# Second-layer outer products by Strassen's seven, SiLU kept in float32, and another pace and order in the decode of w_in2

## The chip, the cores and the metric

One core of a Trainium2 chip runs the whole program as one launch. The metric is the device time of one execution in microseconds (us); lower is better. Every execution quoted here is of the full problem.

## What is computed

```
q,k,v: [4, 8, 1152, 64] float32; two weight pairs: w_in [512, 2048], w_out [2048, 512], float64 bits
q_pool = mean of q over pairs of rows                         # 576 query rows per head
x      = softmax(q_pool @ k^T / 8) @ v, heads side by side    # [2304, 512]
h = x @ w_in1;  x = (h * cos(h)) @ w_out1                     # layer 1
h = x @ w_in2;  out = silu(h) @ w_out2                        # layer 2, [2304, 512]
```

All results are float32. The weights arrive as 64-bit floats and are taken apart bit by bit on the chip.

## The kernel before, in words

**Precision.** Every float32 operand of a large product is scaled by a power of two and split into two float16 tiles, high and low. A product then takes three matmuls on TensorE: high by high, high by low, low by high (line 519 on, `g1_unit`).

**Blocks.** The 2304 tokens go through both layers as 9 blocks of 256 tokens. For a block, `g1_unit` makes one of 16 chunks `f` of the hidden layer, 128 x 256, with 12 matmuls of 256 columns; `g1_evac` (line 533) takes two chunks out of PSUM at a time on ScalarE. In layer 1 `g_cos_begin` and `g_cos_end` (lines 544, 556) make h cos h of four chunks with four VectorE instructions, one ScalarE sine and one GpSimd subtraction, and `g2_unit1` (line 578) the outer product. In layer 2 `g_silu` (line 571) splits the SiLU result of four chunks into float16 halves in the tile `gt`, and `g2_unit2` (line 600) does the outer product of chunk `f`: two halves of 128 tokens by three passes, 6 matmuls of 512 columns, 96 for a block. `y_evac2` (line 612) scales the two PSUM banks of 512 columns out and stores them.

**Order of the tail.** While attention's last batch runs, the decode of layer 2's weights begins. `units = layer1()` (line 656) yields once for each chunk of layer 1; for each such unit the tail's loop (line 902 on) takes one step of `wgen2`, the generator that loads, decodes and splits layer 2's weights, until w_in2 is done. Then the loop over the blocks `n` and the chunks `f` of layer 2 begins (some 20 lines from line 935 on): a `g1_unit`, its evacuation, one more step of `wgen2` (now w_out2), a step of the load of the next block, and, 48 chunks behind, one `g2_unit2`. The outer products therefore start with block 3 and the last three blocks of them run alone at the end.

**Weights.** `weight_steps` (line 155) works in pieces of 1024 columns of float64 on each of 128 partitions: 8 pieces of w_in2 and 8 of w_out2. A piece is one DMA, a `decode` (line 191: one ScalarE absolute value, four wide VectorE instructions, at lines 207, 210, 215 and 218) and a `write` (line 232: ScalarE twice, at lines 238 and 239, GpSimd once, at line 240). The piece's scale comes from `scale_steps` (line 79): two tiny VectorE instructions make `mw` (lines 88, 91), one tiny TensorE matmul spreads it over the partitions as `bm` (line 96), and three more VectorE instructions make the scale of it (lines 99, 103, 107).

Instructions of an engine run in the order in which the scheduler, from the program's order and its priorities, has put them into that engine's queue; a waiting instruction holds back all behind it.

## Time and profile before

| | |
|---|---|
| median of 3 runs | 1407.86 us (1405.83 to 1409.97) |
| the profiled execution | 1411.62 us, of which the span is 1409.8 us |
| granted clock, mean | 0.928 |
| TensorE (PE) busy | 1162.9 us, 82% |
| VectorE (DVE) | 996.4 us, 71% |
| ScalarE (ACT) | 767.5 us, 54% |
| GpSimd (POOL) | 567.2 us, 40% |
| tail of layer 1 | about 866 to 1021 us |
| first blocks of layer 2 | about 1021 to 1100 us |
| layer 2, both products | about 1100 to 1340 us |
| outer products alone | about 1340 to 1403 us |

PE busy over the whole span says little: in attention (before about 850 us) several engines share the work, in the tail PE does nearly all of it. The four stretches of the table are read apart. The granted clock is the share of full speed at which TensorE was let run. PEld is TensorE's weight load, which runs beside its matmuls.

### The profile page before, as it was taken

What the parts mean: (1) busy time and instruction counts of PE and PEld (TensorE: products, weight loads), DVE (VectorE), ACT (ScalarE), POOL (GpSimd) and SP (SyncE); (2) the same over time, 40 slices, a digit from 0 to 9 for tenths busy, and PEclk for the clock granted to TensorE, in tenths of its full rate; (3) what the DMA queues carried; (4) which work ended last, traced back from release to release, by engine and by line L of the source; (5) the groups of instructions that cost most, each with busy time, mean ns of one, the idle gap of its engine ahead of it and who ended that gap; (6) DMA issues with size and microseconds to landing.
All of it is one profiled execution on the core that took longest, in us unless ns stands there. A gap on an engine that the chain in (4) does not pass through costs nothing.

```text
span 1409.8 us, 24849 instructions
## 1 busy us (share of the span) xinstructions
PE 1162.9 (82%) x10020; PEld 852.0 (60%) x10020; DVE 996.4 (71%) x1848; ACT 767.5 (54%) x907; POOL 567.2 (40%) x296
## 2 busy tenths in 40 slices
PE   1465356787988778898889889979989999999998
PEld 0243233475676556666667678868878766666643
DVE  7999997778777888977999885997776323223110
ACT  3686487668777678876788775553363111111100
POOL 1577276535755466645666563552321000000000
PEclk9976568699999989998999999999999999999999
DMA  7799789987799999978899964441330000000001
GB/s 232 192 239 209 188 155 204 202 171 135 154 201 174 202 194 211 177 151 181 152 209 184 214 131 91 151 119 46 90 105 32 16 31 30 16 16 16 1 30 30
DMA packets 493074, 186.16 MB, mean 132 GB/s; under 512 B 433056, under 2 KB 467872, under 8 KB 492960
## 3 DMA queue, kind: packets, MB, share of 16 engines
q1 hardware_dynamic: 492960, 184.59, 61.7%
q8 instruction: 78, 1.28, 0.4%
q14 instruction: 36, 0.29, 0.1%
HBM read 66.58 MB, written 9.44 MB: 54 GB/s over the span
## 4 chain that ended last, share of the span: by engine, by line
PE 36%; DVE 25%; ACT 9%; issue 8%; DMA 7%; POOL 2%; SPq 2%; ACTq 0%; DVEq 0%; POOLq 0%
PE h L527 14%; PE o L607 13%; DVE sc L410 5%; PE y L586 5%; DMA hlT<-hl 3%; DVE tt L553 2%; DVE tt L552 2%; POOL hl L429 2%; PE sp L391 2%; ACT hl L424 2%; SPq L431 2%; PE pv L442 2%; DVE gh L567 1%; DVE tt L562 1%; DVE vt L311 1%
## 5 line engine op out<-in xcount | busy, mean ns | idle before, releaser
L429 POOL TENSOR_TENSOR hl<-sc,hl 128x1152 f16<-128x1152 f32 x144 | 367.8, 2563 | 189.9 <-ACT hl L424 110.8
L391 PE MATMUL sp<-kT,qT 128*128 128x512 f16 (+1 forms) x768 | 197.6, 375 | 111.2 <-DVE sc L410 86.5
L527 PEld LDWEIGHTS <-ih 128*128 128x128 f16 x2304 | 225.8, 99 | 64.6 <-issue 12.5
L410 DVE TENSOR_SCALAR_CACHE_REDUCE sc<-sp,psu 128x512 f32<-128x512 f32 (+1 forms) x288 | 229.2, 807 | 40.2 <-PE sp L391 38.8
L540 ACT ACTIVATE hk<-h,ca 128x512 f32<-128x512 f32 x144 | 97.7, 682 | 255.0 <-PE h L527 251.0
L418 ACT ACTIVATE sc<-sc,nb 128x1152 f32<-128x1152 f32 x144 | 180.3, 1252 | 95.2 <-DVE nb L415 80.6
L442 PE MATMUL pv<-vt,hlT 128*128 128x130 f16 (+1 forms) x1440 | 197.2, 239 | 39.6 <-DMA hlT<-hl 33.3
L527 PE MATMUL h<-ys,ih 128*128 128x256 f16 x1152 | 194.8, 273 | 2.9 <-ACT hk L540 2.7
L442 PEld LDWEIGHTS <-hlT 128*128 128x128 f16 (+1 forms) x1440 | 148.6, 111 | 71.0 <-DMA hlT<-hl 45.4
L527 PE MATMUL h<-xT,ih 128*128 128x256 f16 x1024 | 187.1, 276 | 4.7 <-ACT hk L540 3.9
L446 PE MATMUL pv<-vt,hlT 128*128 128x65 f16 (+1 forms) x1440 | 189.5, 209 | 0.0
L607 PE MATMUL o<-oh,gt 128*128 128x512 f16 x576 | 187.9, 379 | 1.0 <-ACT oh L238 0.6
L391 PEld LDWEIGHTS <-qT 128*128 128x128 f16 x768 | 77.9, 110 | 179.2 <-issue 137.1
L424 ACT ACTIVATE hl<-sc 128x1152 f16<-128x1152 f32 x144 | 165.5, 1157 | 18.5 <-DMA xT<-xn 8.9
L586 PE MATMUL y<-gl,oh 128*128 128x256 f16 x576 | 159.4, 277 | 3.7 <-POOL gl L568 3.7
L586 PE MATMUL y<-gh,oh 128*128 128x256 f16 x576 | 159.8, 277 | 2.5 <-ACT y L595 1.7
L586 PE MATMUL y<-gh,ol 128*128 128x256 f16 x576 | 159.7, 277 | 0.0
L527 PE MATMUL h<-ys,il 128*128 128x256 f16 x576 | 157.0, 273 | 0.0
L446 PEld LDWEIGHTS <-hlT 128*128 128x128 f16 (+1 forms) x1440 | 143.7, 108 | 16.2 <-issue 6.7
L527 PE MATMUL h<-xT,il 128*128 128x256 f16 x512 | 141.5, 276 | 0.0
L568 POOL TENSOR_TENSOR gl<-tt,gh 128x1024 f16<-128x1024 f32 x36 | 93.5, 2598 | 110.2 <-DVE gh L567 105.5
L607 PEld LDWEIGHTS <-gt 128*128 128x128 f16 x864 | 84.6, 98 | 81.3 <-issue 2.1
(281 smaller groups left out, 1884.5 us busy)
## 6 DMA issues: line engine op xcount, KB each, us to landing
wst<-in_moe_w_in_dram SPq DMA_DIRECT2D x16, 1024.0 KB, 5.7
wst<-in_moe_w_out_dram SPq DMA_DIRECT2D x16, 1024.0 KB, 6.2
stk<-in_k_dram SPq DMA_DIRECT2D x32, 288.0 KB, 4.0
stv<-in_v_dram SPq DMA_DIRECT2D x32, 288.0 KB, 4.4
stq<-in_q_dram SPq DMA_DIRECT2D x32, 256.0 KB, 3.1
ydr<-y SPq DMA_DIRECT2D x9, 512.0 KB, 3.8
y32b<-ydr SPq DMA_DIRECT2D x9, 512.0 KB, 3.3
out_dram<-osb SPq DMA_DIRECT2D x16, 256.0 KB, 2.1
```

The source lines that it names most:

```text
L391: nc.tensor.matmul(sp[:, o - a:o - a + n], P.qT[e][:, t, :], kT[:, o:o + n], start=(e == 0), stop=(e == 1))
L410: nc.vector.tensor_scalar(out=T.sc[:, a:z], in0=sp, scalar1=T.P.su, scalar2=None, op0=ALU.mult, op1=ALU.min, accum_out=mx[:, x:x + 1],)
L418: nc.scalar.activation(out=T.sc, in_=T.sc, func=AF.Exp, scale=-1.0, bias=nb)
L424: nc.scalar.activation(out=hi, in_=T.sc, func=AF.Copy)
L429: nc.gpsimd.tensor_tensor(out=T.hl[:, 1, :], in0=T.sc, in1=T.hl[:, 0, :], op=ALU.subtract)
L442: nc.tensor.matmul(G.pv[r, T.gi], T.hlT[:, 0, c, r], P.vt[i][:, c], start=(c == 0), stop=(c == KC - 1), skip_group_check=True,)
L446: nc.tensor.matmul(G.pv[r, T.gi, 0], T.hlT[:, 1, c, r], P.vt[i][:, c, 0], start=False, stop=(c == KC - 1), skip_group_check=True,)
L527: nc.tensor.matmul(hp, wt[:, c, f * 128:(f + 1) * 128], xt(c), start=(i == 0), stop=(i == 3 * NC - 1), skip_group_check=True,)
L540: nc.scalar.activation(out=o, in_=blk.hp, func=AF.Copy if first else AF.Silu, scale=blk.c.a[:, g:g + 1])
L568: nc.gpsimd.tensor_tensor(out=G.gl, in0=t, in1=gh, op=ALU.subtract)
L586: nc.tensor.matmul(blk.y[:, oc, :], wt[:, f, oc * 128:(oc + 1) * 128], gt[:, f % 4, :], start=(f == 0 and e == 0 and oc % 2 == 0), stop=(f ...
L607: nc.tensor.matmul(blk.y[i], gt[:, f % 4, i * 128:(i + 1) * 128], wt[:, f, :], start=(f == 0 and e == 0), stop=(f == NF - 1 and e == 2),)
```

## The change

**Outer products.** `g_silu`, `g2_unit2` and `y_evac2` go. The SiLU result now stays in float32, in a tile `gs` where layer 1's weights were (the fourth block's in smaller freed tiles). A block's outer product, 256 tokens by 2048 by 512, is cut in halves on each axis and done with seven products of 128 tokens by 1024 by 256 columns in place of eight: `outer_operand` makes the seven left operands `a11, a12, s2, s1, s3, a22, s4` (sums of quarters of `gs` on VectorE, then a ScalarE copy for the high half and a VectorE instruction for the low half), `outer_steps` does 8 x 3 matmuls of 256 columns for each, 168 for a block, and adds the products up: in PSUM (banks Y, X and W) and with small ScalarE and VectorE instructions into the tile `o`. Five operands are made ahead (`OP_AHEAD`). The first product starts in block 3 at chunk 8 (`G2_AT`), and 14 half products follow for 16 chunks.

**Right operands.** A piece of w_out2 is now a slice of 32 columns from each half of its 512: two DMAs with runs of 256 bytes in place of one with 512. `write_sums` makes seven tiles of sums from it: four GpSimd subtractions of 256 elements, and high and low halves (one ScalarE scaling and four copies, four GpSimd subtractions of 256 or 512 elements) in place of two ScalarE and one GpSimd instruction of 1024 elements.

**Decode.** Of w_in2 one step of `wgen2` is taken for two units of layer 1 in place of one step for one (`W2_EACH`). And `apart` splits `scale_steps`: `mw` is made at once, but the `bm` matmul and what follows come with the next piece.

**Memory.** PSUM's pool `ps_m` has one bank in place of two. The tile of w_out2's last two sums lies where layer 1's `ih1` was.

Order of VectorE in the tail of layer 1, where pieces of w_in2 (`wt`, `wst`, `mw`, `bm`) and groups of layer 1's cosine (`tt`, `hk`, `gh`) alternate. Before:

```order
L99 TENSOR_SCALAR ui2_113<-bm_10688 128x1
L210 TENSOR_SCALAR wt_10724<-wt_10724 128x1024
L88 TENSOR_SCALAR mw_10756<-wm_10723 128x1
L553 SCALAR_TENSOR_TENSOR tt_10981<-tt_10981,hk_10907 128x1024
L103 TENSOR_SCALAR si2_112<-ui2_113 128x1
L215 SCALAR_TENSOR_TENSOR wst_10625<-wst_10625,wt_10724 128x1024
L91 SCALAR_TENSOR_TENSOR mw_10756<-wm_10723,mw_10756 128x1
L567 CAST gh_10826<-tt_10828 128x1024
L107 TENSOR_SCALAR ui2_113<-ui2_113 128x1
L218 SCALAR_TENSOR_TENSOR wst_10625<-wst_10625 128x1024
L562 SCALAR_TENSOR_TENSOR tt_10981<-hk_10907,ck_10333,tt_10981 128x1024
L99 TENSOR_SCALAR ui2_113<-bm_10759 128x1
```

After (line 96 is now 99, 99 is 102, 207 is 230, 210 is 233, 215 is 238, 218 is 241, 552 is 620, 562 is 630, 567 is 635):

```order
L230 TENSOR_SCALAR wt_10957,wm_10956<-wt_10957 128x1024
L635 CAST gh_10768<-tt_10770 128x1024
L233 TENSOR_SCALAR wt_10957<-wt_10957 128x1024
L89 TENSOR_SCALAR mw_11019<-wm_10956 128x1
L630 SCALAR_TENSOR_TENSOR tt_10903<-hk_10839,ck_10328,tt_10903 128x1024
L238 SCALAR_TENSOR_TENSOR wst_10794<-wst_10794,wt_10957 128x1024
L92 SCALAR_TENSOR_TENSOR mw_11019<-wm_10956,mw_11019 128x1
L102 TENSOR_SCALAR ui2_113<-bm_10989 128x1
L620 TENSOR_SCALAR tt_11037<-hk_10973 128x1024
L241 SCALAR_TENSOR_TENSOR wst_10794<-wst_10794 128x1024
L106 TENSOR_SCALAR si2_112<-ui2_113 128x1
```

Before, `bm_10759` is read (last row) five rows behind `mw_10756`, its own piece's. After, the row behind `mw_11019` reads `bm_10989`, which belongs to the piece before.

Order of GpSimd where w_out2's pieces (`wst`) come last. Before, three pieces with layer 1's last groups between them:

```order
L240 TENSOR_TENSOR ol2_10395<-wst_10932,oh2_10394 128x16x64
L240 TENSOR_TENSOR ol2_10395<-wst_11015,oh2_10394 128x16x64
L568 TENSOR_TENSOR gl_11783<-tt_11784,gh_11782 128x1024
L568 TENSOR_TENSOR gl_11896<-tt_11897,gh_11895 128x1024
L240 TENSOR_TENSOR ol2_10395<-wst_12130,oh2_10394 128x16x64
L240 TENSOR_TENSOR ol2_10395<-wst_12211,oh2_10394 128x16x64
```

After, one piece and the start of the next; `ops5` and `ops2` hold the seven sums, and three of the four subtractions of 256 elements stand in one row:

```order
L284 TENSOR_TENSOR wst_12354<-wst_12354 128x256 x3
L275 TENSOR_TENSOR ops5_10389<-wst_12354,ops5_10389 128x16x32
L275 TENSOR_TENSOR ops5_10389<-wst_12354,ops5_10389 128x8x32
L284 TENSOR_TENSOR wst_12354<-wst_12354 128x256
L275 TENSOR_TENSOR ops5_10389<-wst_12354,ops5_10389 128x16x32
L284 TENSOR_TENSOR wst_12457<-wst_12457 128x256 x2
```

One instruction of 1024 elements for a piece has become eight of 256 or 512.

Order of TensorE where the first products come in. Before, chunk 3 of block 3 (`h`) and the first outer products (`o`) alternate:

```order
L527 MATMUL h_12971<-ys_12795,ih2_10392 128x256
L527 LDWEIGHTS il2_10393
L527 MATMUL h_12971<-ys_12795,il2_10393 128x256
L607 LDWEIGHTS gt_12074
L607 MATMUL o_12944<-oh2_10394,gt_12074 128x512
L527 LDWEIGHTS ih2_10392
L527 MATMUL h_12971<-ys_12795,ih2_10392 128x256
```

After, at chunk 8 of block 3, with `op` the left and `ops5` the right operand, and `oy`, `ox` the banks:

```order
L592 MATMUL h_13073<-ys_12853,il2_10388 128x256
L761 LDWEIGHTS op_13131
L761 MATMUL oy_13150<-ops5_10389,op_13131 128x256
L761 LDWEIGHTS op_13131
L761 MATMUL oy_13150<-ops5_10389,op_13131 128x256
L99 MATMUL bm_13923<-ym_13883,mean_72 128x1
L761 LDWEIGHTS op_13134
L761 MATMUL ox_13208<-ops5_10389,op_13134 128x256
```

Two matmuls of 512 columns with one weight load each have become more of 256 columns, each with its own.

The core of the diff:

```diff
-W2_BUFS, W2_PACE, W2_N = 3, 6, 1
+W2_BUFS, W2_PACE, W2_EACH = 3, 6, 2
+G2_AT, OP_AHEAD = 8, 5
...
-    def scale_steps(m, pool, res, top, wide=False):
+    def scale_steps(m, pool, res, top, wide=False, apart=False):
...
             m = w
+            if apart:
+                yield
         bc = pool.tile([128, 2, GW], F32, tag="h", name="bm")[:, 0, 0:4]
         nc.tensor.matmul(bc[:, 0:n], mean, m, start=True, stop=True)
...
+                if w.sums and kind == "o":
+                    n //= 2
+                    st = stage.tile([128, 2, c, n, z], dt, tag="wst", name="wst", bufs=bufs)
+                    for j in range(2):
+                        o = j * (DM // 2) + p * n
+                        eng.dma_start(
+                            out=st[:, j].rearrange("p c f z -> p c (f z)"),
+                            in_=srcs[1][:, o * z:(o + n) * z].rearrange("(c p) f -> p c f", p=128),
+                        )
...
+        def write_sums(p):
+            st = decoded.pop(0)[0]
+            v, f = (st[:, :, :, z] for z in (1, 0))
+            nc.scalar.activation(out=v, in_=v, func=AF.Copy, scale=w.so[:, p:p + 1])
+            b11, b21, b12, b22 = (v[:, i * (NF // 2):(i + 1) * (NF // 2)] for i in range(4))
+            t1, t3, t2, t4 = (f[:, i * (NF // 2):(i + 1) * (NF // 2)] for i in range(4))
+            for o, x, y in ((t1, b12, b11), (t3, b22, b12), (t2, b22, t1), (t4, b21, t2)):
+                nc.gpsimd.tensor_tensor(out=o, in0=x, in1=y, op=ALU.subtract)
+            halves((0, 2), v[:, 0:NF], p)
+            yield
+            halves((2, 1), b22, p)
+            halves((3, 4), f, p)
+            more()
...
-                nc.tensor.matmul(
-                    blk.y[i], gt[:, f % 4, i * 128:(i + 1) * 128], wt[:, f, :],
-                    start=(f == 0 and e == 0), stop=(f == NF - 1 and e == 2),
-                )
...
+        if op == "s2":
+            s1 = mp.p.tile([128, HF, 128], F32, tag="hk", name="s1", bufs=NB_HK)
+            blk.s1 = lambda c, n: s1[:, c:c + n, :]
+            total(blk.s1, a22, a21, ALU.add, g1)
+            total(a21, a11, a21, ALU.subtract, g0)
+            total(a11, blk.s1, a11, ALU.subtract, g0)
+        elif op == "s4":
+            total(a12, a12, a11, ALU.subtract, g1)
...
+            nc.scalar.activation(out=h, in_=x(c, g), func=AF.Copy, scale=blk.c.k)
+            nc.vector.scalar_tensor_tensor(
+                out=l, in0=x(c, g), scalar=blk.c.k, in1=h, op0=ALU.mult, op1=ALU.subtract
+            )
...
+            bank = B.X if op == "a12" else B.W if op in ("s1", "s4") else B.Y
+            start = op in ("a11", "a12", "s1")
...
+            for c in range(HF):
+                for e, wt in ((0, oh), (0, ol), (1, oh)):
+                    nc.tensor.matmul(bank, t[:, e, c, :], wt[:, c, :], start=start, stop=True, skip_group_check=True)
+                    start = False
...
+            if op == "a11":
+                copy(o[:, 0, d0], bank)
+            elif op == "a12":
+                add(o[:, 0, d0], bank)
+            elif op == "s2":
+                copy(o[:, 0, d1], bank)
+            elif op == "s3":
+                copy(o[:, 1, d1], bank)
+                add(o[:, 1, d1], B.W)
+            elif op == "a22":
+                scaled(B, o[:, 1, d0], bank)
+                scaled(B, o[:, 1, d1], o[:, 1, d1])
+            elif op == "s4":
+                add(o[:, 0, d1], bank)
+                for d in (d0, d1):
+                    scaled(B, o[:, 0, d], o[:, 0, d])
...
+            step += 1
+            if step % W2_EACH == 0 and not W2.half:
+                next(wgen2, None)
...
-                if f % 4 == 3:
-                    g_silu(cur, f)
-                pend.append((cur, f, n))
                 next(wgen2, None)
...
-                if len(pend) > (TAIL_G - 1) * NF:
-                    second()
+                if outer is None and n == TAIL_G - 1 and f == G2_AT:
+                    outer = outer_steps(state.mp, opp, W2, blocks, banks, out_dst, OP_AHEAD)
+                if outer is not None:
+                    credit += 14
+                    while credit >= NF:
+                        credit -= NF
+                        next(outer, None)
```

## Rows read from the trace of the kernel before

**Rows 1.** Chain of waits, 850 to 1410 us: start us, us, what

```profile
1076.78 5.24 PE h L527 x48
...
1383.72 20.89 PE o L607 x96
```

**Rows 2.** Busy us (x instructions) by engine and stretch; granted clock; DMA share; GB/s

```profile
866.00:1021.00 155.00, 140.05 (x1239) 122.45 (x1239) 127.53 (x172) 73.77 (x84) 62.57 (x23) 0.97 0.34 97
1021.00:1100.00 79.00, 73.44 (x647) 63.00 (x646) 52.12 (x83) 36.01 (x46) 12.74 (x5) 1.00 0.20 61
1100.00:1340.00 240.00, 240.00 (x1666) 162.57 (x1665) 66.88 (x94) 36.76 (x51) 0.00 (x0) 1.00 0.05 18
...
890.00:942.00 52.00, 42.35 (x366) 36.10 (x364) 52.00 (x74) 27.99 (x31) 22.41 (x8) 0.93 0.32 94
```

**Rows 3.** What PE waited for, 866 to 1021 us: total us, times, longest

```profile
PE bm L96 <- DVE mw L91: 7.9, 3, 6.7
PE h L527 <- ACT hk L540: 2.9, 3, 2.4
```

**Rows 4.** What PE waited for, 1021 to 1130 us

```profile
PE h L527 <- ACT hk L540: 2.7, 3, 1.3
PE bm L96 <- DVE mw L91: 2.0, 1, 2.0
```

**Rows 5.** Timeline of PE: start us, us, work [idle before, releaser]

```profile
927.61 0.58 PE L96 MATMUL bm<-mw,mean 128*128 128x1 f32 x2 [6.71 <-DVE mw L91]
```

**Rows 6.** Busy time by stretch behind that wait, columns as above

```profile
928.00:930.00 2.00, 2.00 (x11) 1.44 (x12) 2.00 (x5) 0.70 (x1) 0.00 (x0) 0.50 0.00 0
930.00:932.00 2.00, 2.00 (x15) 1.59 (x14) 2.00 (x7) 1.16 (x1) 0.00 (x0) 0.72 0.00 0
```

**Rows 7.** DVE by line, 890 to 942 us: xcount, busy us, mean ns

```profile
L562 DVE SCALAR_TENSOR_TENSOR tt<-hk,ck,tt 128x1024 f32<-128x1024 f32 x5 | 10.1, 2012 | 0.0
L210 DVE TENSOR_SCALAR wt<-wt 128x1024 int32<-128x1024 int32 x6 | 8.7, 1444 | 0.0
```

**Rows 8.** Timeline of DVE, one clean row at 930 us

```profile
929.99 0.69 DVE L210 TENSOR_SCALAR wt<-wt 128x1024 int32<-128x1024 int32 x1
```

**Rows 9.** Timeline of POOL, about 1000 us

```profile
999.45 4.68 POOL L240 TENSOR_TENSOR ol<-wst,oh 128x1024 f16<-128x1024 f32 x2 [5.59 <-ACT wst L239]
```

**Rows 10.** Timeline of DVE beside it, and one like it at 990 us

```profile
990.65 1.22 DVE L553 SCALAR_TENSOR_TENSOR tt<-tt,hk 128x1024 f32<-128x1024 f32 x1
...
1002.17 3.04 DVE L553 SCALAR_TENSOR_TENSOR tt<-tt,hk 128x1024 f32<-128x1024 f32 x1
```

**Rows 11.** POOL by line, 1021 to 1100 us

```profile
L240 POOL TENSOR_TENSOR ol<-wst,oh 128x1024 f16<-128x1024 f32 x5 | 12.7, 2554 | 41.7 <-ACT wst L239 41.7
```

**Rows 12.** Timeline of POOL, an undisturbed row near the start

```profile
5.63 1.40 POOL L316 TENSOR_TENSOR stq<-stq 128x576 f32<-128x576 f32 x1 [4.48 <-DMA stq<-in_q_dram]
```

**Rows 13.** ACT by line and shape, 866 to 1100 us

```profile
L595 ACT ACTIVATE y<-y,cy 128x256 f32<-128x256 f32 x16 | 6.4, 476 | 7.6 <-PE y L586 5.2 <-POOL gl L568 2.4
L890 ACT ACTIVATE ys<-y32b,ys 128x1024 f16<-128x1024 f32 x4 | 4.6, 1148 | 0.0
```

**Rows 14.** DVE by line and shape, 1021 to 1410 us

```profile
L575 DVE SCALAR_TENSOR_TENSOR gt<-hk,ck,gt 128x1024 f16<-128x1024 f32 x36 | 46.2, 1282 | 0.9
...
L617 DVE TENSOR_TENSOR osb<-o,cy 128x512 f32<-128x512 f32 x18 | 12.3, 689 | 106.7 <-PE o L607 106.7
```

**Rows 15.** The page's DMA issues: KB each, median us to landing

```profile
wst<-in_moe_w_in_dram SPq DMA_DIRECT2D x16, 1024.0 KB, 5.7
wst<-in_moe_w_out_dram SPq DMA_DIRECT2D x16, 1024.0 KB, 6.2
```

**Rows 16.** Timeline of DVE at the end

```profile
1403.99 1.34 DVE L617 TENSOR_TENSOR osb<-o,cy 128x512 f32<-128x512 f32 x2 [19.68 <-PE o L607]
```

**Rows 17.** Timeline of SP's DMA queue at the end

```profile
1404.71 2.46 SPq L622 DMA_DIRECT2D out_dram<-osb  x4
```

**Rows 18.** The page's groups: PE weight loads of line 527

```profile
L527 PEld LDWEIGHTS <-ih 128*128 128x128 f16 x2304 | 225.8, 99 | 64.6 <-issue 12.5
```

More of the change, by code (lines that the diff above doesn't have):

```diff
@@ L147, in new_w @@
         w.half = False
+        w.sums = sums
         for nm in ("si", "ui", "so", "uo"):
@@ L220, in decode @@
                 )
-                ts.append(st.bitcast(F32)[:, :, :, 1])
+                ts.append(st.bitcast(F32) if w.sums and kind == "o" else st.bitcast(F32)[:, :, :, 1])
+                for g in rest:
+                    next(g)
                 yield
+            for g in rest:
+                run_all(g)
             m1 = m
@@ L226, in decode, with halves @@
                 nc.vector.tensor_reduce(out=m1, in_=m, axis=AX.X, op=ALU.max)
-            for _ in early(scale_steps(m1, pspool(), (s, u), 14, wide), P_CH):
-                pass
+            g = early(scale_steps(m1, pspool(), (s, u), 13 if w.sums and kind == "o" else 14, wide, apart), P_CH)
+            if apart:
+                next(g)
+                scaling.append(g)
+            else:
+                run_all(g)
             decoded.append(ts)
             yield
+        def halves(ops, t, p):
+            o, n = ops
+            f = t.shape[2]
+            for x0, x1, hi, lo in w.ops:
+                y0, y1 = max(o, x0), min(o + n, x1)
+                if y0 >= y1:
+                    continue
+                h, l = (
+                    x[:, y0 - x0:y1 - x0].rearrange("p o c f -> p (o c) f")[:, :, p * f:(p + 1) * f] for x in (hi, lo)
+                )
+                tt = t[:, (y0 - o) * (NF // 2):(y1 - o) * (NF // 2)]
+                nc.scalar.activation(out=h, in_=tt, func=AF.Copy)
+                nc.gpsimd.tensor_tensor(out=l, in0=tt, in1=h, op=ALU.subtract)
+        def write_sums(p):
[11 more added lines that the diff above has]
+            more()
+            yield
         def write(kind, p):
+            if w.sums and kind == "o":
+                yield from write_sums(p)
+                return
             c, n = shape(kind)
@@ L255, in weight_steps @@
                 yield from decode(*pieces[i + ahead])
+            else:
+                finish_scales()
             yield from write(*x)
-        r = npc // NC
+        r = 0 if w.sums else npc // NC
         for e in range(r):
@@ L536, in g1_evac @@
         g = f * w.npc // NF
-        if f % 4 == 1:
-            blk.hk = mp.p.tile([128, 4, GW], F32, tag="hk", name="hk", bufs=NB_HK)
-        o = blk.hk[:, (f % 4) - 1:(f % 4) + 1, :]
+        if first:
+            if f % 4 == 1:
+                blk.hk = mp.p.tile([128, 4, GW], F32, tag="hk", name="hk", bufs=NB_HK)
+            o = blk.hk[:, (f % 4) - 1:(f % 4) + 1, :]
+        else:
+            o = blk.view(f - 1, 2)
         nc.scalar.activation(
@@ L612, in y_evac2, with __init__, view @@
-    def y_evac2(W2, pool, blk, dsts):
-        cy = y_scale(W2, blk.u, W2.uo, "cy0")
-        for i in range(2):
-            o = pool.tile([128, DM], F32, tag="x32_%d" % i, name="osb")
-            np_ = W2.npc
+    class Slot:
+        def __init__(self, parts):
+            self.parts = parts
+        def view(self, c, n):
+            for c0, n0, t in self.parts:
+                if c0 <= c and c + n <= c0 + n0:
+                    return t[:, c - c0:c - c0 + n, :]
+    HF = NF // 2
+    PRODUCTS = ("a11", "a12", "s2", "s1", "s3", "a22", "s4")
@@ new lines, in outer_steps, with prepare, copy, add @@
+    def outer_steps(mp, opp, w, blocks, banks, dsts, ahead_n):
+        seq = [(0, "a11")]
+        for n in range(len(blocks)):
+            seq += [(n, op) for op in ("a12", "s2", "s1", "s3")]
+            if n + 1 < len(blocks):
+                seq.append((n + 1, "a11"))
+            seq += [(n, "a22"), (n, "s4")]
+        todo = list(seq)
+        ready = []
+        def prepare(k):
+            while todo and len(ready) < k:
+                n, op = todo[0]
+                if blocks[n] is None:
+                    return
+                todo.pop(0)
+                ready.append(outer_operand(mp, opp, blocks[n], op))
+        def copy(o, x):
+            nc.scalar.activation(out=o, in_=x, func=AF.Copy)
+        def add(o, x):
+            nc.vector.tensor_tensor(out=o, in0=o, in1=x, op=ALU.add)
+        def scaled(B, o, x):
+            np_ = w.npc
@@ L925, in attention_moe_moe_kernel, with banks @@
         cur = yb.blk
-        pend = []
-        def second():
-            blk, ff, nn = pend.pop(0)
-            g2_unit2(W2, blk, ff, ps_o)
-            if ff == NF - 1:
-                y_evac2(W2, wpool, blk, out_dst(nn))
-        gen = None
+        blocks = [None] * NB
+        def banks(nm, n):
+            if nm == "Y":
+                t = ps_o.tile([128, DM], F32, tag="o%d" % (n % 2), name="oy")
+            elif nm == "X":
+                t = ps_y.tile([128, NC, GW], F32, tag="y", name="ox").rearrange("p c n -> p (c n)")
+            else:
+                t = ps_m.tile([128, DM], F32, tag="w", name="ow")
+            return t[:, 0:DM // 2]
+        outer = None
+        credit = 0
         for n in range(NB):
@@ L955, in attention_moe_moe_kernel @@
                 cur = nyb.blk
-        while pend:
-            second()
+        run_all(outer)
         ctx.enter_context(moe_stack)
```

119 lines of the change are left out of this document (86 added, 33 removed).

## The prediction

> **What bounds the kernel now.** I read the chain of waits first, then busy time by stretch, then who waited for whom inside the stretches that are not full. The chain from 1100 us on is TensorE (PE) and nothing else: its pieces are runs of layer 2's first product, 48 matmuls of 256 columns in 5.24 us, and of the outer product, 96 matmuls of 512 columns in 20.89 us [rows 1]. That is 109.2 ns and 217.6 ns for one, and the first pair of numbers to keep. By stretch, PE is busy 240.00 of 240 us between 1100 and 1340, so there only PE work counts. Between 866 and 1021 it is busy 140.05 of 155, which leaves 15 us idle, and between 1021 and 1100 it is busy 73.44 of 79, which leaves 5.6 [rows 2]. What PE waited for in the first of these is the little matmul `bm` of a weight piece's scale, 7.9 us in 3 waits, one of 6.7, and a free `hk`, 2.9 us [rows 3]; in the second `hk` again, 2.7 us, and `bm`, 2.0 us [rows 4]. A long wait costs twice: behind the 6.71 us wait [rows 5] the granted clock is 0.50 (1.2 of 2.4 GHz) for two us and 0.72 for two more [rows 6], so 2 x 0.50 + 2 x 0.28 = 1.6 us are lost on top. What PE waits for is VectorE (DVE): it is busy all 52.00 us between 890 and 942 [rows 2], and its instructions are stretched there. A decode instruction of line 210 has a mean of 1444 ns [rows 7] against 0.69 us where nothing disturbs it [rows 8]. While GpSimd (POOL) ran two subtractions in 4.68 us [rows 9], DVE's line 553 took 3.04 us instead of 1.22 [rows 10]: the two hold each other up.
>
> **A, the products.** Per block 96 x 217.6 ns = 20.89 us go, and 7 x 8 x 3 = 168 matmuls of 256 columns come. Their nearest row is line 527, of the same shape, types and pattern of one weight load for each matmul: 168 x 109.2 ns = 18.35 us. So a block saves 2.54 us, and nine save **22.9 us**, all of it on the path: the outer products run either where PE is always busy or alone at the end. The weight loads go from one for 512 columns to one for 256; a load takes 99 ns in line 527's groups [rows 18], less than the 109.2 ns of a matmul, and lies beside it there already. Here a rule speaks against the change. The Trainium skill ("TensorE: Matmul & The Clock Gate", section Back-to-back issue gap) gives about 131 ns for a matmul of 512 columns in a stream with a weight load each, and 81 ns for one of 128. By that, as an estimate between its two figures, 256 columns take some 98 ns, and 1512 x 98 ns less 864 x 131 ns makes the products 35 us slower instead. The rows do not agree with it, 217.6 and 109.2 ns, and the measurement decides.
>
> New operands need other engines. A block takes 7 low halves on DVE like line 575's 1282 ns, 4 sums of 1024 elements like the 1.22 us row, and 7 small output instructions of 256 elements at a bit over half of line 617's 689 ns [rows 10, 14], taken as 0.42: 9.0 + 4.9 + 2.9 = 16.8 us, for 18.35 us of PE work. ScalarE (ACT) takes 7 copies like line 890's 1148 ns and 3 of 256 columns like line 595's 476 [rows 13]: 9.5 us. Both fit, DVE not by much. In the stretch to 1340 half of the PE time is the first product's, so there the fit is easy; DVE has 66.88 of 240 us busy now [rows 2]. I cost this work at nothing. Its cover is five operands made ahead; without it every product would show an operand's ACT and DVE time.
>
> **B, the decode of w_in2 and the late scale.** In the order of DVE `bm` is now read one piece behind its `mw`, so PE issues that matmul long after its input is there: the 7.9 us of waits should go, and with them the 1.6 us of clock; a good half of `hk`'s 2.9 could, with about as much of the clock, 1.5 us, behind its wait of 2.4. At most 7.9 + 1.6 + 2.4 + 1.5 = 13.4 us. At least nothing: DVE is full in 890 to 942, and a wait that leaves PE's `bm` can come back at `hk` or `gh`. The two orders differ less than the halved rate says, since both have about one piece for each group of cosine; 9 pieces stand beside 9 groups before, beside 10 after. A tenth of the stretch's DVE work of 52 us is 5 to 6 us. I take 6 us for that and 2 for the clock: **8 us**, nearer the middle than either end, because the wait is surely removed and its cause, a full DVE, only eased.
>
> **C, the new right operands and the first products.** Two rows of the stretch 1021 to 1100 show what changes: the `bm` wait of 2.0 us goes [rows 4], but POOL's work for a piece grows. Now it is one subtraction of 2554 ns [rows 11]. A bare subtraction of 576 elements takes 1.40 us [rows 12], so four of 256 take some 0.7 to 0.9 each and four halves of 256 to 512 some 4.4 in all, 7.2 to 8.3 us for a piece. With 5 such pieces left in that stretch POOL's 12.7 us become 36 to 42, of the 41.7 + 12.7 it has there, so it still fits. But POOL holds up DVE longer, and SP's queue now carries 16 DMAs for w_out2 instead of 8. The first product must have the last piece's sums, and its first operand lies where the last sums' staging was: from that piece POOL's 7 to 8 us and then 1.15 + 1.28 us for the operand. It stands at chunk 8 of block 3 in PE's order, 56 x 12 x 109.2 ns = 73.4 us behind the first matmul of layer 2, where the old one stood at chunk 3. No row shows the price. If all fits, the stretch's idle 5.6 us go but for half a microsecond: -5. If POOL is one and a half pieces late, +12. I take **+3**: the pieces come closely packed, as POOL's fill of 36 to 42 of 54 us says, and half a late piece less the gone `bm` wait is about that.
>
> **D, the end.** Behind the last matmul DVE now multiplies twice, 512 elements each, 1.34 us together [rows 16], and the first store goes out after 0.7. With the change an addition and two scalings of 256 elements stand before the first store, three by 0.42 in a row, about 1.3 us; the stores' own 2.46 us [rows 17] stay. I take **+0.7**, between 0 and +1.2.
>
> **The sum.** -22.9 - 8 + 3 + 0.7 = -27.2. The profiled execution took 1411.6 us, so 1384.4; it lies 3.8 above the median of the runs, 1407.9, to which I refer the forecast: **1381 us**, or 1380.7 before rounding. The ends of the parts give 22.9 + 13.4 + 5 = 41.3 less, 1367, and 22.9 - 12 - 1.2 = 9.7 less, 1398.
>
> **Rivals.**
> *Better than forecast.* The whole 13.4 us of B go, and C brings 4: -22.9 - 13.4 - 4 + 0.7 = -39.6, **1368 us**. For it speaks that the `bm` wait is more than half of the idle time; against it that DVE has no slack there.
> *DVE stays the bound.* The waits only change their name, B is 0, and POOL's sums are late, C is +6: -16.2, **1392 us**. The full 52 us and the stretched instructions speak for it.
> *Short runs.* The rows have w_in2's pieces landing after 5.7 us and w_out2's, with runs of 512 bytes, after 6.2 [rows 15]; runs of 256 bytes have no row. If a piece takes twice 6.2 us, the eight pieces fall behind by up to 50 us, of which the 41.7 us that POOL sits idle there take most: about +8, **1389 us**. The Trainium skill ("DMA: Bandwidth & Descriptors", section Specifications) asks for 512 bytes and more for full rate; no run here shows a shorter run's rate. Against it: two of the three staged pieces are loaded ahead.
> *A wait at every change of product, slower than before.* There are 63 products, and each needs an operand from ACT and DVE and a bank that ACT or DVE has copied out (Y again for `s2`, `s3` and `a22`, W for `s4`, and now one bank in `ps_m`). It decides from 27.2 / 63 = 0.43 us for each. The nearest waits of PE for ACT are 2.7 us in 3 [rows 4], 0.9 each; then 63 x 0.9 = 57 us come on top: **1437 us**. Against it: a product runs 2.62 us, the copy of a bank takes half of one, and Y only gets more added to it.
> *The matmuls are dearer than line 527's.* At 864 x 217.6 / 1512 = 124.3 ns each nothing is left of A and the sum is -4.3, **1404 us**. Only a weight load longer than 109 ns would do it, against 99 in the row.
>
> **How the numbers follow.** I give the forecast 0.59, better 0.08, DVE as bound 0.17, short runs 0.10, a wait at every product 0.04, dearer matmuls 0.02. A measurement here tells from no change what is over 0.3%, 4.2 us, so "faster" ends at 1403.6. The first four cases are faster, though the last two of them together, or with a late start, would reach 1400, so I leave some of them to "same": faster 0.91, same 0.04, slower 0.05. The range takes in the forecast, DVE as bound, short runs and the edge of the better case: 1367 to 1397. It leaves out the two slower rivals and the worst end of C.
>
> **What would show it.** Right: 1512 matmuls of 256 columns at 109 ns in the new products, the last 24 and a half of them (126 half products less the 77 that fit in beside the first product) alone at the end for 64 us without gaps, `bm` waits of under 3 us in all, DVE with some idle time in the tail of layer 1. Wrong: PE idle before the new products that wait for `op` or for a bank, more than 6 us idle where the first of them stands, waits for `hk` and `gh` as long together as `bm`'s were, or w_out2's pieces landing after 9 us or more.

## The result

The changed kernel takes 1397.68 us at the median (1395.49 to 1400.23, 4 runs) against 1407.46 (1405.83 to 1409.97, 4 runs): a ratio of 0.9913 with a 95% interval of [0.9884, 0.9943]. It is faster, by 9.8 us where 27 were forecast, and 0.7 us outside the range of 1367 to 1397. Measured again with more runs it came to 1393.42 us against 1411.69, a ratio of 0.9869 [0.9845, 0.9893], so 18 us; what is known of the difference stands among the experiments. The profiled execution took 1400.23 us, of which the span is 1398.1.

First the same cuts in both traces, at places that mean the same: the end of attention, the last `y` of layer 1, the first outer product, the last first product `h`, the last outer product. Busy time by stretch of the kernel before:

```profile
859.60:1021.20 161.60, 146.65 (x1301) 128.46 (x1300) 133.54 (x191) 75.75 (x88) 64.70 (x24) 0.97 0.33 95
1021.20:1064.30 43.10, 37.54 (x338) 32.77 (x337) 33.65 (x63) 25.16 (x31) 10.62 (x4) 1.00 0.32 96
1064.30:1340.30 276.00, 276.00 (x1973) 192.80 (x1973) 85.15 (x116) 47.61 (x67) 2.12 (x1) 1.00 0.05 18
1340.30:1404.60 64.30, 63.89 (x294) 28.55 (x292) 6.64 (x10) 0.68 (x1) 0.00 (x0) 1.00 0.07 25
```

and of the changed kernel; columns as in [rows 2]:

```profile
865.30:1030.00 164.70, 148.72 (x1308) 130.06 (x1307) 124.27 (x181) 73.97 (x91) 78.01 (x37) 0.97 0.35 87
1030.00:1111.90 81.90, 74.13 (x673) 65.08 (x671) 45.69 (x88) 48.73 (x70) 52.17 (x48) 1.00 0.32 78
1111.90:1327.30 215.40, 215.40 (x1978) 193.07 (x1976) 114.05 (x158) 89.40 (x122) 0.00 (x0) 1.00 0.05 18
1327.30:1393.50 66.20, 65.64 (x600) 58.44 (x598) 42.02 (x67) 26.56 (x42) 0.00 (x0) 1.00 0.08 28
```

Length less PE busy is PE's idle time. Up to the last `y` it was 161.6 - 146.65 = 15.0 us and is 164.7 - 148.72 = 16.0: the stretch that was to give 8 us has become 3.1 us longer, 1.0 of it idle time and 2.1 PE's busy time. Seven more of layer 2's matmuls stand in it, some 0.8 us, and the rest goes with the clock: the mean granted clock is 0.97 in both, but before, 3.3 us of the time at 0.50 (1.2 of 2.4 GHz) lay in PE's idle time, and now PE is busy in all of it. The 2 us that B was to give by the clock did not come. Up to the first product idle time goes from 5.6 to 7.8 us. Then PE is full in both. PE's busy time behind the last `y` falls from 37.54 + 276.00 + 63.89 = 377.4 us to 74.13 + 215.40 + 65.64 = 355.2, by 22.3: that is part A, but for the 0.8 us of those seven matmuls. The end behind the last matmul takes 1398.1 - 1393.5 = 4.6 us in place of 5.2. Together, behind the end of attention: 550.2 us before, 532.8 now, **17.4 less**. But in these two executions attention ended at 859.6 and at 865.3.

What PE waits for up to the last `y`, in the changed kernel:

```profile
PE h L592 <- ACT hk L608: 7.2, 4, 3.6
PE y L647 <- POOL gl L636: 5.2, 3, 3.1
PE bm L99 <- DVE si L106: 1.7, 1, 1.7
PE y L647 <- ACT y L656: 1.0, 1, 1.0
PE bm L99 <- DVE mw L92: 0.8, 1, 0.8
```

Against [rows 3] `bm` fell from 7.9 us to 1.7 + 0.8, as forecast; `hk` rose from 2.9 to 7.2 and `gl` from 2.3 to 5.2. From the last `y` to the first product:

```profile
PE h L592 <- ACT gs L608: 7.2, 8, 1.4
PE bm L99 <- DVE mw L92: 0.6, 1, 0.6
```

The waits of [rows 4] are replaced by eight for `gs`, the evacuation of SiLU.

Where `hk` comes from is read in three timelines about the longest of these waits. PE:

```profile
950.29 0.44 PE L592 MATMUL h<-xT,ih 128*128 128x256 f16 x2 [3.63 <-ACT hk L608]
```

ScalarE, which has to evacuate that `hk`:

```profile
947.46 1.20 ACT L301 ACTIVATE ih<-wst,si 128x1024 f16<-128x1024 f32 x1 [3.81 <-DVE si L106]
948.57 1.10 ACT L229 ACTIVATE wt<-wst 128x1024 f32<-128x1024 f32 x1
949.56 0.68 ACT L608 ACTIVATE hk<-h,ca 128x512 f32<-128x512 f32 x1
```

VectorE:

```profile
946.08 0.15 DVE L102 TENSOR_SCALAR ui<-bm 128x1 f32<-128x1 f32 x1
946.15 1.22 DVE L241 SCALAR_TENSOR_TENSOR wst<-wst 128x1024 int32<-128x1024 int32 x1
947.28 0.15 DVE L106 TENSOR_SCALAR si<-ui 128x1 int32<-128x1 int32 x1
```

The late scale is there: `bm`, of the piece before, is read at 946.08. But the scale `si` is made of it only behind another wide bit instruction, at 947.28; ScalarE's write of that piece (L301) stood waiting for `si` since 943.66; the absolute value of the next decode (L229) follows, then `hk` at 949.56, and PE waits 3.63 us for that. **The wait of PE for a scale has become a wait of ScalarE for the scale made of it, with PE's evacuation queued behind.** The next longest, 2.66 us for `hk` at 936.64, has the same order: ScalarE stood 6.95 us for `si`, while two VectorE instructions ahead of it took 3.08 and 3.15 us in place of 1.2, beside two subtractions on GpSimd. ScalarE's waits for `si` up to the last `y`, before and now:

```profile
ACT ih L238 <- DVE si L103: 7.7, 3, 4.1
...
ACT ih L301 <- DVE si L106: 11.5, 3, 7.0
```

GpSimd's work from the end of attention to the first product, by line and shape:

```profile
L636 POOL TENSOR_TENSOR gl<-tt,gh 128x1024 f16<-128x1024 f32 x13 | 36.3, 2795 | 43.7 <-DVE gh L635 34.5 <-DVE ui L110 7.2 <-DVE mw L89 2.0
L284 POOL TENSOR_TENSOR wst<-wst 128x256 f32<-128x256 f32 x32 | 35.7, 1134 | 32.1 <-ACT wst L280 32.1
L275 POOL TENSOR_TENSOR ops<-wst,ops 128x512 f16<-128x512 f32 x24 | 31.7, 1326 | 3.8 <-ACT ops L274 3.8
...
L275 POOL TENSOR_TENSOR ops<-wst,ops 128x256 f16<-128x256 f32 x8 | 8.3, 1043 | 0.0
```

The eight pieces of w_out2 take 35.7 + 31.7 + 8.3 = 75.7 us, 9.5 each, where its one subtraction took 2.55 before [rows 11]. And ScalarE from the last `y` to the first product:

```profile
ACT ops L274 <- POOL wst L284: 18.0, 9, 3.7
ACT gs L608 <- PE h L592: 6.4, 5, 2.3
```

It waits 18.0 us for GpSimd's subtractions (line 284), at the copy of a high half (line 274), while a `gs` stands behind that copy. One such place, two rows of ScalarE and one of PE:

```profile
1063.43 0.67 ACT L274 ACTIVATE ops<-wst 128x512 f16<-128x512 f32 x1 [3.53 <-POOL wst L284]
1064.00 1.25 ACT L608 ACTIVATE gs<-h,ca 128x512 f32<-128x512 f32 x2
...
1064.72 0.38 PE L592 MATMUL h<-ys,ih 128*128 128x256 f16 x2 [1.38 <-ACT gs L608]
```

### The profile page after: what moved, and what is told of

It is laid out like the page before. It is cut to its first block, busy times and chain, and to the rows that moved or that the text cites. A ratio compares the mean times of both kernels' runs of the same rounds, so it can differ in the third digit from the quotient of the medians.

```text
span 1398.1 us, 26495 instructions
## 1 busy us (share of the span) xinstructions
PE 1145.2 (82%) x10668; PEld 916.7 (66%) x10668; DVE 1065.5 (76%) x1958; ACT 856.6 (61%) x1045; POOL 619.3 (44%) x352
## 4 chain that ended last, share of the span: by engine, by line
PE 31%; DVE 22%; ACT 9%; POOL 9%; issue 8%; DMA 7%; SPq 3%; POOLq 0%; ACTq 0%; DVEq 0%
PE h L592 11%; PE oy L761 7%; DVE sc L475 5%; PE ow L761 3%; PE y L647 3%; DVE tt L621 3%; POOL hl L494 2%; POOL ops L275 2%; DMA hlT<-hl 2%; POOL wst L284 2%; ACT hl L489 2%; PE sp L456 2%; DVE tt L620 2%; PE ox L761 2%; POOL gl L636 2%
## 5 line engine op out<-in xcount | busy, mean ns | idle before, releaser
L592 PE MATMUL h<-xT,ih 128*128 128x256 f16 x1024 | 190.1, 279 | 11.0 <-ACT hk L608 10.4
L761 PEld LDWEIGHTS <-op 128*128 128x128 f16 x1512 | 147.9, 98 | 17.8 <-issue 0.6
L592 PE MATMUL h<-ys,il 128*128 128x256 f16 x576 | 157.0, 273 | 0.0
L647 PEld LDWEIGHTS <-oh 128*128 128x128 f16 x1152 | 113.0, 100 | 20.9 <-issue 4.5
L592 PEld LDWEIGHTS <-il 128*128 128x128 f16 x1152 | 114.0, 99 | 16.7 <-issue 1.5
```

Of the source, the lines that this page charges most:

```text
L592: nc.tensor.matmul(hp, wt[:, c, f * 128:(f + 1) * 128], xt(c), start=(i == 0), stop=(i == 3 * NC - 1), skip_group_check=True,)
L647: nc.tensor.matmul(blk.y[:, oc, :], wt[:, f, oc * 128:(oc + 1) * 128], gt[:, f % 4, :], start=(f == 0 and e == 0 and oc % 2 == 0), stop=(f ...
L761: nc.tensor.matmul(bank, t[:, e, c, :], wt[:, c, :], start=start, stop=True, skip_group_check=True)
```

## The experiments

**Theory Q** is that the gain was given back in queues: GpSimd's sums of w_out2 come ahead of `gl` on GpSimd, and ScalarE's copies, which wait for them, ahead of `hk` and `gs`. **Theory D**, the rival (not part D of the sum): VectorE's load sets the pace of the tail, and a wait taken away only changes its name. All runs at a glance; lengths and idle times from one profile each, cut as above, "behind" from the end of attention to the end of the span, the ratio of the runs against those of the kernel before:

| kernel | attention ends | to last y | PE idle there | PE idle to first product | behind | ratio |
|---|---|---|---|---|---|---|
| before | 859.6 | 161.6 | 15.0 | 5.6 | 550.2 | |
| changed | 865.3 | 164.7 | 16.0 | 7.8 | 532.8 | 0.9913 |
| changed again | 855.7 | 166.4 | 17.7 | 8.3 | 535.1 | 0.9869 |
| e1 decode part alone | 858.9 | 162.4 | 13.8 | 3.0 | 547.4 | 0.9991 |
| e2 pace of before | 861.4 | 164.9 | 16.6 | 7.7 | 533.0 | 0.9875 |
| e3 scale at once | 858.1 | 161.7 | 13.7 | 13.1 | 537.7 | 0.9899 |
| e4 sums on VectorE | 856.1 | 160.7 | 12.4 | 8.9 | 531.7 | 0.9883 |
| e5 no sums | 861.0 | 160.2 | 11.8 | 2.9 | 522.6 | 0.9804 |
| e6 halves later | 856.3 | 163.5 | 15.5 | 8.3 | 533.6 | 0.9890 |
| e7 short decode | 865.6 | 157.0 | 11.6 | 5.0 | 522.0 | 0.9826 |
| e9 scale sooner | 859.7 | 163.3 | 16.2 | 7.8 | 531.5 | 0.9890 |
| e10 e9, highs on VectorE | 858.4 | 164.9 | 19.0 | 7.2 | 535.1 | 0.9890 |
| e11 e9, sums' highs on VectorE | 861.3 | 164.3 | 18.1 | 6.2 | 533.3 | 0.9876 |
| e12 sums on both | 861.5 | 160.8 | 14.0 | 9.6 | 536.0 | 0.9889 |
| e13 short decode, no sums | 861.9 | 154.1 | 9.3 | 1.5 | 514.9 | 0.9779 |
| e14 before, short decode | 861.3 | 158.7 | 12.6 | 2.2 | 542.2 | 0.9942 |

**The changed kernel again.**

> The changed kernel again, unchanged. In seven profiles so far the end of attention lay between 856 and 865 us although its instructions are the same; the changed kernel's own profile had the latest. If that is chance: attention ends at 856 to 861 us, the stretch behind it is again within 1 us of 532.8, and the runs come to 14 to 18 us faster than before. If the change slows attention: it ends at 864 us or later again, 8 to 11 us faster than before.

Attention ended at 855.7 us and the runs came to 18 us less. The same kernel gave 865.3 and 855.7, and over all profiles the end of attention lies between 855.7 and 865.6 us. TensorE's first 5,724 matmuls, most of attention, run in the same order before and after; the last of them starts at 823.3 us in the kernel before, and in the changed one at 828.7 and, this time, at 819.1. So the difference is not the change's; what makes it is not known. Behind attention the two executions are 17.4 and 15.1 us shorter than the kernel before, so the 18 us of this measurement lie nearer to what the change is worth than the 9.8 of the first. Kernels are compared behind attention; there the same kernel gave 532.8 and 535.1, and less than about 3 us tells nothing.

**e1, the decode part alone**, on the kernel before:

```diff
-W2_BUFS, W2_PACE, W2_N = 3, 6, 1
+W2_BUFS, W2_PACE, W2_EACH = 3, 6, 2
...
+            if apart:
+                yield
```

> The kernel before with only the decode part of the change: one step of w_in2's decode for two units of layer 1, and the scale's matmul a piece later; outer products and w_out2 as before. Theory Q (queues: the decode part helps by itself, and what it gains is given back because GpSimd's new sums of w_out2 sit in the queues of GpSimd and ScalarE ahead of layer 1's gl and layer 2's evacuations): PE's idle time between the end of attention and the last y falls from 15 us to 7 to 9, waits for bm under 3 us, the whole 5 to 8 us faster than before. Theory D (VectorE sets the pace of that stretch, the waits only change their names): idle stays at 14 to 17 us, bm's 7.9 us turn up at hk and gl, the whole within 2 us of before.

Behind attention 2.8 us less than before, and a ratio of 0.9991 [0.9975, 1.0008]. PE's waits up to the last `y`:

```profile
PE h L546 <- ACT hk L559: 6.1, 3, 2.7
PE y L605 <- ACT y L614: 5.4, 2, 4.5
PE y L605 <- POOL gl L587: 1.3, 2, 0.9
PE bm L98 <- DVE mw L91: 1.0, 1, 1.0
```

`bm` went from 7.9 us to 1.0; `hk` went from 2.9 to 6.1 and the wait for ScalarE's `y` from 1.0 to 5.4. The longest, 4.5 us for `y`, ends at 954.82. On ScalarE that `y` stands behind a write that waits for `si`:

```profile
952.09 1.23 ACT L255 ACTIVATE ih<-wst,si 128x1024 f16<-128x1024 f32 x1 [2.12 <-DVE si L105]
953.22 1.55 ACT L614 ACTIVATE y<-y,cy 128x256 f32<-128x256 f32 x4
```

That is theory D's picture, in a kernel without w_out2's sums. Part B was small by itself; it wasn't only given back.

**e2 and e3, one part of it undone** in the changed kernel:

```diff
-W2_BUFS, W2_PACE, W2_EACH = 3, 6, 2
+W2_BUFS, W2_PACE, W2_EACH = 3, 6, 1
```

> The changed kernel with one step of w_in2's decode for each unit again. Theory Q: bm's waits stay under 3 us since the scale still comes a piece later; GpSimd's sums of w_out2 come no later, the whole within 3 us of the changed kernel. Theory D: more VectorE work beside each group of cosine: waits for hk and gl together grow from 12.4 us by 3 to 6, the stretch up to the last y as much longer.

```diff
-..., nc.sync, 1, W2_BUFS, 1, 1, True)
+..., nc.sync, 1, W2_BUFS, 1, 1)
```

> The changed kernel with the scale's matmul at once again, the slow pace kept. Theory Q: bm's waits are back at 6 to 9 us in the stretch up to the last y, hk and gl stay at 12, the whole 4 to 7 us slower than the changed kernel. Theory D: bm's waits are back, but hk's and gl's fall by as much; idle time of the stretch 14 to 18 us as in both kernels, the whole within 2 us of the changed kernel.

The pace is worth nothing, 533.0 us: `bm` waits 7.2 us again, `hk` 3.7 in place of 7.2, `gl` 4.6. Both theories missed there, as theory D wanted `hk` and `gl` longer and Q `bm` short. Without the late scale it is 3 to 5 us longer behind attention. Up to the last `y` it is 3 to 5 us shorter; behind it PE waits 6.0 us for one `bm` and 5.3 us for one `ys`, the split of layer 2's input on VectorE, and for `gs` only 1.8. So if the late scale is worth anything in this kernel, it is not where I put it; the runs (0.9899 against 0.9913 and 0.9869) show no difference.

**e4, the sums on VectorE:**

```diff
-                nc.gpsimd.tensor_tensor(out=o, in0=x, in1=y, op=ALU.subtract)
+                nc.vector.tensor_tensor(out=o, in0=x, in1=y, op=ALU.subtract)
```

> The changed kernel with the four subtractions of 256 elements for each piece of w_out2 on VectorE in place of GpSimd. Theory Q: ScalarE's half copies no longer wait 18 us for these subtractions, PE's waits for gs fall from 7.2 us to under 3, those for gl from 5.2 to about 3: 5 to 8 us faster than the changed kernel. Theory D: 32 more VectorE instructions of about 0.4 us stand in the engine that sets the pace: the stretch up to the last y gets longer by 1 to 3 us, the waits for gs fall by less than half, the whole between 3 us slower and 2 us faster.

Between the two. `gl`'s waits fell from 5.2 us to 1.7, as Q said, and the tail's idle time to 12.4; but `gs` kept 6.7 + 0.5, since ScalarE's copies now waited 11.6 us for VectorE's subtractions. The subtractions took 788 ns each at the mean there, where about 0.4 us had been expected. The place moved and the queue stayed: 1 to 3 us less in all.

**e5, the sums left out,** and **e7, a shorter decode:**

```diff
-            for o, x, y in ((t1, b12, b11), (t3, b22, b12), (t2, b22, t1), (t4, b21, t2)):
-                nc.gpsimd.tensor_tensor(out=o, in0=x, in1=y, op=ALU.subtract)
...
-            halves((3, 4), f, p)
+            halves((3, 4), v, p)
```

> The changed kernel without the four GpSimd subtractions of each w_out2 piece (the four sums' tiles are filled with plain quarters instead). Theory Q: ScalarE's half copies then wait for nothing on GpSimd, PE's waits for gs fall from 7.2 us to under 2, those for gl from 5.2 to 3 or less; the stretch behind attention 6 to 9 us shorter than 532.8. Theory D (VectorE sets the pace, GpSimd's sums matter little): waits for gs fall by less than half, the stretch up to the last y keeps its 14 to 16 us idle; 0 to 3 us shorter.

```diff
-                nc.vector.scalar_tensor_tensor(
+                apart or nc.vector.scalar_tensor_tensor(
                     out=v, in0=st[:, :, :, 0], scalar=29,
```

> The changed kernel without the last of the four wide VectorE instructions of a decode of layer 2's weights (their lowest three bits are left out), 1.2 us less VectorE work for each piece. Theory D: up to the last y VectorE has some 10 pieces less 1.2 us, and PE's idle time there falls from 16 us by 5 or more. If the waits there come from GpSimd's and ScalarE's queues instead (Q): it falls by less than 3.

(`apart` is true for layer 2's weights alone.) These two decide. Without the sums the stretch behind attention is 10 to 12.5 us shorter. Up to the last `y` and up to the first product PE waits for

```profile
PE h L590 <- ACT hk L606: 7.2, 4, 3.6
PE bm L99 <- DVE mw L92: 2.5, 2, 1.7
PE y L645 <- POOL gl L634: 1.1, 2, 0.6
```

```profile
PE h L590 <- ACT gs L606: 2.0, 3, 1.1
```

`gl` 5.2 to 1.1 and `gs` 7.2 to 2.0: Q's two waits are the sums', and `hk`, which is not, stays at 7.2. With 1.2 us less of VectorE for a piece it is 11 to 13 us shorter, and `hk`, `gl` and `gs` all fall (5.2, 3.1, 4.1). Up to the last `y`:

```profile
865.60:1022.60 157.00, 145.41 (x1309) 127.99 (x1307) 110.80 (x172) 73.62 (x91) 75.61 (x37) 0.99 0.37 91
```

PE's idle time fell by 4.4 to 6.1 us, and its busy time, for as many matmuls, by 3.3, at a granted clock of 0.99 in place of 0.97. Theory D holds as well. By the medians of the runs both effects are smaller: against the kernel before, the changed kernel gains 18.3 us, e5 27.0 and e7 23.6, so 8.7 and 5.3 us more. The profile of e7 has the latest end of attention of all, 865.6 us; how much of its 11 to 13 us is that one execution stays open.

**e6, the halves a step later:**

```diff
             halves((2, 1), b22, p)
+            yield
             halves((3, 4), f, p)
```

> The changed kernel with a piece's halves of the sums one step of the generator (one chunk of layer 2) behind its subtractions. Theory Q: the copies find most sums made, ScalarE's 18 us of waits for GpSimd fall under 8 and PE's waits for gs from 7.2 under 4; 3 to 5 us shorter behind attention. Theory D: no difference over 1.5 us.

`gs` fell to 4.5, `bm` came with 3.5; 533.6 us, no gain. ScalarE's waits for the subtractions did not fall under 8 us as theory Q wanted; they are 19.6.

**e9 to e11, the scale sooner, and high halves on VectorE.**

```diff
+                for g in rest:
+                    next(g)
                 nc.vector.tensor_scalar(
                     out=t, in0=t, scalar1=W_MIN,
...
+                for g in rest:
+                    run_all(g)
                 yield
...
-                for g in rest:
-                    next(g)
                 yield
-            for g in rest:
-                run_all(g)
```

e10 and e11 add to it

```diff
-                nc.scalar.activation(out=h, in_=tt, func=AF.Copy)
+                nc.vector.tensor_copy(h, tt)
```

for all seven tiles (e10) or for the four sums (e11).

> The changed kernel with the late scale half a piece less late: the bm matmul and the three small instructions behind it are written ahead of the next piece's two wide bit instructions in place of behind them. If the wait for bm turned into ScalarE's wait for si (11.5 us in the stretch up to the last y) with the evacuation hk queued behind it: ScalarE's waits for si fall under 7 us, PE's waits for hk from 7.2 to under 4, the stretch behind attention 2 to 4 us shorter than the changed kernel's 533 to 535. If VectorE's mere load decides: hk's waits are spread elsewhere and the stretch is within 1.5 us.

> The kernel with the sooner scale, and all high halves of w_out2's seven tiles copied by VectorE in place of ScalarE. Theory Q: nothing stands ahead of the SiLU evacuations in ScalarE's queue that waits for GpSimd, so PE's waits for gs fall from 7.2 to 7.7 us to under 2.5; 4 to 6 us shorter behind attention than the kernel with the sooner scale alone. If VectorE's load decides: waits for gl and bm grow by as much, within 2 us of it.

> As the kernel before this one, with only the high halves of the four sums on VectorE and those of the three plain quarters left on ScalarE. Theory Q: the same waits for gs, under 3 us, with less work on VectorE: as fast as that kernel or 1 to 2 us faster. If VectorE's load decides: in between the two kernels.

e9's waits of ScalarE for `si` fell from 11.5 us to 7.2, and PE's for `hk` only from 7.2 to 6.4, while `gl` took 6.6; the stretch was as long as before. So a scale that comes sooner does not free the evacuations: the queue behind `si` is one form of the wait and not its cause. In e10 and e11 `gs` fell to 0.8 and 1.3, as theory Q has it, and `bm` took up 3.4 and 4.0. None of the three is shorter by more than the 3 us that tell.

**e12, the sums on both engines,** two of the four in one instruction of 512 elements on GpSimd, the others on VectorE:

```diff
-            for o, x, y in ((t1, b12, b11), (t3, b22, b12), (t2, b22, t1), (t4, b21, t2)):
-                nc.gpsimd.tensor_tensor(out=o, in0=x, in1=y, op=ALU.subtract)
+            nc.gpsimd.tensor_tensor(out=f4[:, 0:2], in0=v4[:, 2:4], in1=v4[:, 0:4:2], op=ALU.subtract)
+            for o, x, y in ((t2, b22, t1), (t4, b21, t2)):
+                nc.vector.tensor_tensor(out=o, in0=x, in1=y, op=ALU.subtract)
```

> The changed kernel with two of the four sums of a piece made by one GpSimd instruction of 512 elements, the other two by VectorE. GpSimd loses about 2.2 us of 7.5 a piece, VectorE gains 0.8. If the total work of the two engines sets the pace: 3 to 5 us shorter behind attention than the changed kernel's 533 to 535. If only VectorE does: 0 to 2 us longer.

536.0 us, longer by 1 to 3. The two engines' work did not fall by the 1.4 us for a piece that the expectation counts on: from the end of attention on, GpSimd's instructions for the sums took 58.7 us in place of 75.7, 2.1 less for a piece, but VectorE's 16 subtractions took 15.3 us, 1.9 for a piece:

```profile
L286 DVE TENSOR_TENSOR wst<-wst 128x256 f32<-128x256 f32 x16 | 15.3, 955 | 1.0 <-POOL wst L284 0.8
```

So this run is no test of less work in total.

**e13, both cuts, and e14, the short decode in the kernel before** (`w.tag2` is true for layer 2's weights):

> The changed kernel with both cuts: no last wide instruction of the decode (the lowest three bits of layer 2's weights left out) and no GpSimd subtractions for w_out2's sums (plain quarters instead). If they are two limits that add up: 20 to 24 us shorter behind attention than 533 to 535, PE's idle time up to the last y at 7 or less. If one shared limit that either cut already lifts: 11 to 15 us shorter, idle time 10 or more.

```diff
-                nc.vector.scalar_tensor_tensor(
+                w.tag2 or nc.vector.scalar_tensor_tensor(
                     out=v, in0=st[:, :, :, 0], scalar=29,
```

> The kernel before, with the last wide instruction of layer 2's decode left out in the same way. If VectorE's load set the pace already before the change: the stretch from the end of attention to the last y falls from 161.6 us by 5 to 8. If it was the single wait for bm: it stays within 2 us.

Against 534, the mean of the changed kernel's two, both cuts give 19 us; e5 gave 11.4 and e7 12.0, which add up to 23. By the runs e13 gains 31.5 us on the kernel before, 13.2 more than the changed kernel, where e5 and e7 add up to 14. Both lie between what one shared limit and two separate ones would give, and nearer to two. Up to the last `y`:

```profile
861.90:1016.00 154.10, 144.78 (x1308) 127.93 (x1307) 112.73 (x176) 73.39 (x91) 64.68 (x29) 0.99 0.38 93
```

PE is idle for 9.3 us there even so. In the kernel before, the short decode gives 8.0 us behind attention, 2.9 of it up to the last `y` and 3.4 in the idle time that follows; the runs give 6.9. The 2.9 are less than the 5 to 8 that were expected if VectorE's load set the pace, and more than the 2 of a single wait. VectorE's load was a limit there already, `bm`'s three waits one of its forms; of their 7.9 us these are left:

```profile
PE bm L96 <- DVE mw L91: 5.8, 3, 2.9
```

## Why the prediction was wrong

**The direction was right and the size was not; the step that failed is B.** It took 8 us, "because the wait is surely removed and its cause, a full DVE, only eased". The wait was removed (7.9 to 2.5), and e1 shows what that is worth: 1.2 us of idle time up to the last `y`, 2.8 behind attention, nothing in the ratio. The rest came back as `hk` and `y`, waits whose releaser is ScalarE but whose cause is VectorE, by way of `si`, `tt` and ScalarE's order. I had named that as B's lower end, 0, and then took a middle value. I also let B stand apart from C: in the order of GpSimd the subtractions of two pieces stand among layer 1's last `gl`, and I counted all their cost behind the last `y`. They made PE's waits for `gl` 3 us longer. So the stretch came to +3.1 where -8 was taken, 11.1 us; of the 9.8 that are missing from the sum (27.2 - 17.4) that is more than all, since C and D gave some back. e5 splits it: without the sums the stretch is 160.2 us, 1.4 shorter than before, so 6.6 us are B itself and 4.5 the sums ahead of the last `y`, which C did not count (one profile each). Luck has a part in the number and not in the step: the first measurement missed the range by 0.7 us, the second, 1393.42 us, lies inside it, and B failed in both executions (164.7 and 166.4 us up to the last `y`).

**A was right to within 1.5 us.** 22.3 us less PE work behind the last `y` for 22.9, of which some 0.8 are the seven matmuls that now stand ahead of it. The products run as rows of line 527 do:

```profile
L761 PE MATMUL oy<-ops,op 128*128 128x256 f16 x864 | 103.1, 273 | 0.5 <-ACT osb L730 0.5
L761 PE MATMUL ow<-ops,op 128*128 128x256 f16 x432 | 51.7, 273 | 0.0
L761 PE MATMUL ox<-ops,op 128*128 128x256 f16 x216 | 26.2, 273 | 0.0
```

864 + 432 + 216 = 1512 matmuls, with 0.5 us of waits. (The mean of 273 ns is the whole passage of one matmul; they overlap.) The last 600 took 65.64 us alone, 109.4 ns each, where 64 us were forecast for 588. No weight load showed as time of PE. The Trainium skill's figures for a stream of matmuls ("TensorE: Matmul & The Clock Gate", Back-to-back issue gap), by which this part was to cost 35 us, did not hold here: 109.4 ns against the estimate of 98 for 256 columns, and 217.6 [rows 1] against 131 for 512. The wait at each of 63 products did not come: VectorE is busy 42.02 of the last 66.20 us and kept ahead. No run took away the five operands made ahead, so their share in that is not shown.

**C had the right size by another way.** The idle time to the first product grew by 2.2 us for +3. No product came late. The cost is ScalarE's queue: 18.0 us of waits for sums, 7.2 us of PE's for `gs`; e5 takes the first away and leaves 2.0 of the second. GpSimd needs 9.5 us for a piece, where 7.2 to 8.3 were worked out (the terms given there add up to 8.0 at most).

**D was -0.6 for +0.7.** VectorE's instructions at the end take 0.42 us each, as taken; but two and not three of them stand behind the last matmul, and the stores start at 1391.28 us, with the half that is complete by then, ahead of the last matmul's end at 1393.5.

**The rivals.** "DVE stays the bound" comes nearest: it had B at 0, sums late on GpSimd and -16.2 us, against -17.4 behind attention and -9.8 and -18.3 in the two measurements. I gave it 0.17. Short runs fell:

```profile
wst<-in_moe_w_in_dram SPq DMA_DIRECT2D x16, 1024.0 KB, 5.9
...
wst<-in_moe_w_out_dram SPq DMA_DIRECT2D x16, 512.0 KB, 6.5
```

A piece of w_out2 is now two of the second kind, issued together, 6.5 us to landing for 6.2 [rows 15]. ScalarE does wait for these loads, 10.2 us once and 2.4 twice, but no long wait of PE stands behind them.

**What stays open.** Where exactly VectorE and GpSimd hold each other up was not separated from the order of their queues: less work on either (e5, e7) gives 10 to 13 us in the profiles and 5 to 9 in the runs, but moving work from one to the other (e4, e12) gives 3 us at most, and no run took away the mutual hold-up alone. The one bank less in `ps_m` was not tested alone either; no wait of PE in the changed kernel names it. Of kernels that keep all bits of the result none beat the changed one. e7, at 0.9826 [0.9799, 0.9853], is faster than both, at the price of the lowest three bits of layer 2's float32 weights.

## What to carry to other kernels

Price a wait that is removed by what stands next in the waiting engine's queue and by the load of the engine that made it late: while that one is full, the wait returns under another name, and here only less work on it counted (e7, 5 us by the runs, 11 to 13 in the profile) and not a later or smoother order of the same work (e1, e2, e9, 0 to 4). When an instruction is split and spread over engines, look at what is queued behind each new waiting copy: here ScalarE's copies, 0.4 to 0.7 us each, waited 18 us for GpSimd, and PE waited 7.2 us for the evacuations behind them. The work saved on the engine that is full, counted in matmuls of a measured shape, was the reliable part of the sum.
